# A linear-attention, cosine feed-forward and soft mixture-of-experts chain on one Trainium2 core: 256-column groups taken by pairs in one PSUM bank, and weight conversions and small steps in other slots

## The chip, the cores and the metric

One core of a Trainium2 chip runs the whole program. The metric is device time in microseconds of one execution. The profile adds the time on each engine: TensorE (PE, with PEld for its weight loads), VectorE (DVE), ScalarE (ACT), GpSimd (POOL) and the queue of SyncE (SP), which issues nearly all DMAs.

## The reference, cut to what matters

```python
kv  = einsum('bhsd,bhse->bhde', k, v)          # 8 batches, 8 heads, 576 tokens, 64 dims
out = einsum('bhsd,bhde->bhse', q, kv)
x   = out / sqrt(mean(out*out, -1) + 1e-6) * g_norm        # 4608 tokens x 512
h   = x @ w_in                                              # 512 -> 2048
x   = (h * cos(h)) @ w_out                                  # 2048 -> 512
logits = x @ phi                                            # 32 slots
d = softmax(logits over tokens);  c = softmax(logits over slots)
slot_input = d.T @ x                                        # 8 experts x 4 slots x 512
slot_out[e] = relu(slot_input[e] @ w1[e]) @ w2[e]           # 512 -> 1024 -> 512
return c @ slot_out
```

The inputs w_in and w_out come as 64-bit floats and are rebuilt as 32-bit floats on the core by bit operations.

## The kernel before

**Blocks and slots.** The 4608 tokens are taken in ten blocks (SIZES, L67): blocks 0 to 7 of 512 tokens, blocks 8 and 9 of 256. In each block the 2048 hidden features are 16 groups of 128, and "slot (j, f)" is the place of group f of block j in the program. main (L367) makes one group: 12 matmuls into one of three PSUM banks with the tag h (four steps of 128 rows, each as three products of a high and a low part of w_in and x). In blocks 8 and 9 a group uses 256 of the 512 columns of its bank.

**The chain of a group.** turns (L390, ACT) takes h in turns as an integer, rest (L393, DVE) the fraction, cosine (L397, ACT) the cosine, cos_c (L427, DVE) the product gT = h cos(h) in a buffer of a ring (ring_next, L414). gT then goes two ways. logits (L483) and logits2 (L491, blocks 0 and 1) multiply it with wp, which is w_out times phi. For the slot inputs tokens must be on partitions: either DVE transposes 32x32 squares (L437) and regroup (L468) collects them by DMAs from SP and POOL, or, where on_pe (L363) says so (block 0, half of block 1, the last half of block 9), gtr (L454) transposes on PE and ACT copies. slot_acc (L574) adds up d.T @ g over a block into a PSUM bank "ab". w_out itself is applied only at the end, to the 32 sums.

**The order of the work** is written out by hand. Engines run their instructions in program order. Side work is put at slots by at2 (run after main of that slot), late2 (after the first half of the chain), end2 (after the chain) and ld_at (before main; mostly DMA issues on SP). Two lists of tokens give the start: PLAN["start"] (L36) up to the first group, then PLAN["one"] for slots 0 to 3 of block 0 and PLAN["two"] for the slots in which block 0 and block 1 run side by side (block 1 four slots later). From there a loop (L1075) runs one group after the other.

**Conversions.** For each of 16 groups the steps A (cv_scale, ACT), R, P, L (cv_rest, cv_top, cv_low, all DVE), H (cv_hi, ACT) and S (cv_lo, POOL) rebuild w_in; capital letters in the token lists. Small letters a, r, p, l do the first four for w_out transposed (first written by load_wout, L281), from which wp_kk (L322) and wp_sum (L331) make wp. In slot f the group f + 2 of both is converted (LI and LO, L32 and L33), and wp_kk(f) and wp_sum(f) run in slots f and f + 1. w_in 0 and 1 and w_out 0 and 1 are converted in the start list. logits2 of block 0 run two groups at a time in slots 3, 5, ... 17. In blocks 3 to 6 the steps nat_load to nat_store (L338 to L359) rebuild w_out once more in its natural form and put it in DRAM; four of 16 per block, each with the load two slots ahead of nat_scale (ACT).

**Attention** of block j + 1 is made in block j: kv_pair (L183), att_out (L203: ops matmuls, squares on ACT, sums on DVE, power -0.5 on POOL, L220), att_xs (L223, DVE), att_xT (L231, PE and ACT) and att_lo (L246, DVE). In the start the same steps run for block 0, and for block 1 in slots 1 to 4. All of them use four PSUM banks with the tag at (at_bank, L137), which wps, tr, lr, ab and others share.

**The end of a block.** l_evac, l_add, l_max and l_exp (slots 18 and 19, that is slots 2 and 3 of the next block; l_exp makes ACT load another function table and load the old one back), l_T at 21 and slot_acc at 22 (23 and 26 in block 8).

**Expert weights.** fill and fill_kv (L655, L659) load w1 and w2 (128 pieces of 256 KB) into any buffer that has come free, from slot (7, 8) on to the tail, in a fixed order on SP; load_wo2 reads the natural w_out back. tail (L711) runs the experts and writes 12 output tiles of 768 KB.

Of the kernel before, what the change touches and what calls it, by code (L numbers as in the profile page):

```python
# [46 lines left out]
    lg=6,  # L47
    le=18,
    la=19,
    lx=(3, 1),  # L50
    lT=21,
# [3 lines left out]
    K=((0, (0, 0, 0, 0)), (1, (1, 3, 5, 7)), (1, (10, 12, 15, 18))),  # L55
    KL=(((0, 1), (1, 2), (1, 4), (1, 6)), ((1, 8), (1, 11), (1, 13), (1, 16))),
# [19 lines left out]
def tile_linear_attention__ffn_cos__soft_moe(  # L76
# [76 lines left out]
    def load_q(j, t):  # L153
        if j == 0:
            if t == 0:
                first["q"] = g_p.tile([128, TT[0], 4, 128], F32, tag="g1", name="q")
            q_t[j, t] = first["q"][:, t]
        else:
            q_t[j, t] = q_p.tile([128, 4, 128], F32, tag=f"q{(T0[j] + t) % 3}", name="q")
        nc.sync.dma_start(out=q_t[j, t], in_=qT[T0[j] + t])  # L160

    def load_kv(b, pr):
        if b == 1:
            t = kv_all[:, 1] if pr == 3 else first["kv"][pr]
        else:
            t = kv_all[:, 3 if b in (2, 3) else pr]
# [100 lines left out]
    def stage():  # L267
# [99 lines left out]
    def main(j, f):  # L367
        ps = ps_m.tile([128, 512], F32, tag="h", name="h")[:, 0:SIZES[j]]
# [45 lines left out]
    def ring_next(j, f):  # L414
        if (j, f) == (SMALL, 0):
            ring[:] = [[r[0], r[1][:, a:a + 256], 2 * r[3], r[3]] for k in range(2) for r in ring
                       if r[3] == k and r[2] != 1 for a in (0, 256)]
        i = next(i for i, r in enumerate(ring) if (r[0] not in gT_t or j == NB - 1)
                 and (not r[2] or r[2] == 1 and (j == 0 or j == 1 and f < 10) or r[2] == 2 and (j, f) < (SMALL, 2)))
# [71 lines left out]
    def logits2(j, f):  # L491
        if (j, f) == (0, 0):
# [377 lines left out]
    for j in range(NB):  # L870
# [282 lines left out]
```

## Time and profile before

| | us |
|---|---|
| three runs | 719.93, 721.88, 728.15 (median 721.88) |
| the profiled execution: its own time | 718.57 |
| its span in the profile | 716.6 |
| PE busy in the span | 673.7 (94%) |
| DVE busy | 509.6 (71%) |
| ACT busy | 339.0 (47%) |
| POOL busy | 225.7 (32%) |

Busy shares are averages over stages with different limits. A row of the timeline is a stretch of alike instructions with its start and duration; the chain of waits gives the pieces of the path that ended last; the table by stretches gives busy time, the granted clock of PE (1.00 is the upper level, 0.50 the lower), and the share of time in which the 16 DMA engines were busy. The 1.97 us between span and execution time lie outside what the profile shows.

### The profile page before, as it was taken

To read this page: it belongs to the slowest core of one execution; us is meant where nothing else is said; L and a number is where in the kernel's file an instruction comes from. 1 tells how busy PE (TensorE), PEld (TensorE's weight loads), DVE (VectorE), ACT (ScalarE), POOL (GpSimd) and SP (SyncE) were. 2 spreads that over 40 slices of the span, in tenths; PEclk is the share of its full clock that TensorE was granted. 3 is DMA by queue.
4 is the path that set the end of the run, shared out by engine and by line. 5 is a ranking of instruction groups with operands and counts; after the bars stand their busy time and mean duration, and the time that the engine had idled before them with its cause. 6 is when DMAs were issued, how large, how long until landed. Compare 5 with 4: busy or idle time off the path is not lost.

```text
span 716.6 us, 12698 instructions
## 1 busy us (share of the span) xinstructions
PE 673.7 (94%) x4578; PEld 492.2 (69%) x4578; DVE 509.6 (71%) x941; ACT 339.0 (47%) x635; POOL 225.7 (32%) x337
## 2 busy tenths in 40 slices
PE   7868999999999999999999999999999989799994
PEld 6656777776657776677677677766767768674363
DVE  3896888876577768877887877788776666644144
ACT  3564666634453444445443543543454454551143
POOL 3551111211075343441633333344423513110500
PEclk9998999999999999999999999999999999999996
DMA  9973444212185645764786376455509558999998
GB/s 332 326 245 115 147 160 165 74 44 64 37 196 121 175 133 131 211 150 141 173 236 165 86 194 177 134 150 139 124 15 241 134 185 249 342 340 410 393 394 354
DMA packets 73070, 136.18 MB, mean 190 GB/s; under 512 B 11184, under 2 KB 39472, under 8 KB 72240
## 3 DMA queue, kind: packets, MB, share of 16 engines
q1 hardware_dynamic: 65584, 120.16, 52.6%
q0 software_dynamic: 7424, 15.22, 9.3%
q8 instruction: 36, 0.59, 0.3%
q14 instruction: 26, 0.21, 0.1%
HBM read 91.29 MB, written 13.63 MB: 146 GB/s over the span
## 4 chain that ended last, share of the span: by engine, by line
PE 58%; DVE 18%; DMA 10%; ACT 7%; issue 4%; SPq 1%; POOL 0%; DVEq 0%; ACTq 0%; POOLq 0%
PE h L374 35%; DMA kv<-in_w_out 4%; PE ab L585 4%; DVE gT L427 4%; ACT tmp L397 3%; DVE tmp L393 3%; PE ops L208 3%; DVE tr L437 2%; PE l L488 2%; PE kvps L189 2%; PE eh L737 2%; DVE ss L217 2%; PE tr L457 2%; PE xTps L239 2%; PE l L497 1%
## 5 line engine op out<-in xcount | busy, mean ns | idle before, releaser
L374 PE MATMUL h<-xt,w 128*128 128x512 f32 (+1 forms) x1920 | 427.7, 377 | 11.5 <-DVE gT L427 7.6
L374 PEld LDWEIGHTS h<-xt,w 128*128 128x128 f32 x1920 | 332.7, 190 | 99.3 <-issue 18.3
L397 ACT ACTIVATE tmp<-tmp,hpi 128x512 f32<-128x512 f32 (+1 forms) x160 | 108.8, 681 | 172.5 <-DVE tmp L393 172.4
L476 POOL DMA_DIRECT2D g<-tr x232 | 128.3, 556 | 115.4 <-DVE tr L437 45.6
L427 DVE TENSOR_TENSOR gT<-tmp,h 128x512 f32<-128x512 f32 (+1 forms) x152 | 95.8, 630 | 77.8 <-ACT tmp L397 77.4
L220 POOL TENSOR_TENSOR ri<-ss,mhalf 128x8 f32<-128x8 f32 x36 | 60.0, 1672 | 221.7 <-DVE ss L218 214.8
L393 DVE SCALAR_TENSOR_TENSOR tmp<-h,tmp 128x512 f32<-128x512 f32 (+1 forms) x160 | 99.3, 621 | 23.1 <-ACT tmp L390 22.2
L390 ACT ACTIVATE tmp<-h 128x512 int32<-128x512 f32 (+1 forms) x160 | 87.5, 547 | 54.8 <-PE h L374 53.8
L437 DVE STREAM_TRANSPOSE tr<-gT 128x512 f32<-128x512 f32 (+1 forms) x128 | 84.4, 661 | 6.0 <-DMA g<-tr 0.5
L318 POOL TENSOR_TENSOR w<-st_m,w 128x512 fp32r<-128x512 f32 x16 | 23.7, 1479 | 77.4 <-ACT w L313 77.4
L585 PE MATMUL ab<-g,d 128*32 128x512 f32 x256 | 39.9, 594 | 1.3 <-DVE d L561 1.2
L208 PE MATMUL ops<-kvA,q 128*128 128x128 f32 (+1 forms) x320 | 38.8, 280 | 0.2 <-DVE xt L252 0.2
L208 PEld LDWEIGHTS ops<-kvA,q 128*128 128x128 f32 (+1 forms) x320 | 34.3, 180 | 4.4 <-issue 2.5
L243 ACT ACTIVATE xt<-xTps,gn 128x512 fp32r<-128x512 f32 x36 | 24.4, 683 | 24.6 <-PE xTps L239 23.1
L252 DVE SCALAR_TENSOR_TENSOR xt<-xTps,gn,xt 128x512 fp32r<-128x512 f32 x36 | 26.5, 735 | 7.9 <-ACT xt L243 7.6
L217 DVE TENSOR_REDUCE ss<-sq 128x8 f32<-128x512 f32 x32 | 21.7, 679 | 12.4 <-ACT sq L215 12.3
L585 PEld LDWEIGHTS ab<-g,d 128*32 128x32 f32 x256 | 12.7, 109 | 25.9 <-issue 19.5
L215 ACT ACTIVATE sq<-ops 128x512 f32<-128x512 f32 x32 | 19.1, 596 | 24.0 <-PE ops L208 23.0
L488 PE MATMUL l<-gT,wp 128*32 128x512 f32 (+1 forms) x248 | 30.2, 559 | 0.0
L189 PEld LDWEIGHTS kvps<-kv 128*64 128x64 f32 x464 | 16.0, 137 | 11.2 <-issue 8.6
L227 DVE TENSOR_TENSOR sq<-ops,ri 128x512 f32<-128x512 f32 x32 | 21.5, 677 | 2.4 <-POOL ri L220 2.4
L239 PE MATMUL xTps<-ident,sq 128*128 128x128 f32 x128 | 20.5, 287 | 0.4 <-DVE sq L227 0.4
(159 smaller groups left out, 626.5 us busy)
## 6 DMA issues: line engine op xcount, KB each, us to landing
kv<-in_kv SPq DMA_DIRECT2D x29, 512.0 KB, 6.7
g<-tr SPq DMA_DIRECT2D x232, 64.0 KB, 3.6
g<-tr POOLq DMA_DIRECT2D x232, 64.0 KB, 3.5
ew<-in_w SPq DMA_DIRECT2D x25, 512.0 KB, 9.9
q<-in_qT SPq DMA_DIRECT2D x36, 256.0 KB, 3.7
out<-ot SPq DMA_DIRECT2D x12, 768.0 KB, 6.5
rw<-in_w_in SPq DMA_DIRECT2D x16, 512.0 KB, 5.9
kv<-in_w_out SPq DMA_DIRECT2D x16, 512.0 KB, 8.4
```

What stands on the lines that cost most here:

```text
L208: nc.tensor.matmul(out=ps[p0:p0 + n, pr * 128:(pr + 1) * 128], lhsT=q_t[j, t][:, pr, p0:p0 + n], rhs=kvbd[b % 2][:, pr, :], start=True, st ...
L217: nc.vector.tensor_reduce(out=ss, in_=sq, axis=AX.X, op=ALU.add)
L220: nc.gpsimd.tensor_tensor(out=ri[:, :, 0], in0=ss, in1=mhalf, op=ALU.pow)
L374: nc.tensor.matmul(out=ps, lhsT=w[:, a, kk, :], rhs=x[:, b, kk, :], start=(n == 0), stop=(n == 3 * KD - 1))
L390: nc.scalar.activation(out=t.bitcast(I32), in_=ps, func=AF.Copy, bias=0.25, scale=INV_2PI)
L393: nc.vector.scalar_tensor_tensor(out=t, in0=ps, scalar=INV_2PI, in1=t.bitcast(I32), op0=ALU.mult, op1=ALU.subtract)
L397: nc.scalar.activation(out=t, in_=t, func=AF.Sin, bias=hpi, scale=TWO_PI)
L427: nc.vector.tensor_tensor(out=g, in0=fr, in1=h_t.pop((j, f)), op=ALU.mult)
L437: nc.vector.transpose(out=tr_t[j, q][:, :, i, :], in_=gT_t[j, n * q + i].rearrange("p (b t) -> p b t", t=32))
L476: (nc.gpsimd if b % 2 else nc.sync).dma_start(out=dst[32 * b:32 * b + 32, :, x, a:a + n, :].rearrange("p t f i -> p t (f i)"), in_=src[32 ...
L488: nc.tensor.matmul(out=l_t[j][32 * o:32 * o + 32, :], lhsT=wp[:, f, :], rhs=gT_t.pop((j, f)), start=(c == 0), stop=(c == (2 if j == NB - 1 ...
L585: nc.tensor.matmul(out=ps[32 * c:32 * c + 32, :], lhsT=d[:, t, :], rhs=gs[c // 2][t][:, (c % 2) * 512:(c % 2) * 512 + 512], start=(t == 0) ...
```

## The change

What it does:

- Blocks 8 and 9: groups f and f + 1 (f even) share one PSUM bank, 256 columns each. Both mains run, each with its loads and side work, then one chain of 512 columns makes both gT. One DVE instruction transposes both. The ring keeps its 512-column buffers, and both tmp buffers stay in use to the end, so the fill of tmp1 moves from (8, 5) to the tail.
- w_out conversions: no small letters are left in the start list. Group w is converted in slot co[w], from 3 to 13, with two groups in slots 5, 7, 9, 11 and 13. wp_kk and wp_sum follow 2 and 3 slots later, logits2 of block 0 in slots l0. Four gT of block 0 get buffers in the unused half of the q tile.
- Start: the first w_in tile is loaded ahead of k and v, and converted before the first kv_pair; w_in 1 after the last att_lo instead of between them.
- Blocks 2 to 7: the last logits at slot 17 instead of 18, evacuation, maximum, exponential and l_T one slot earlier each (block 7: l_T at 23, slot_acc at 26).
- The natural w_out: three groups per block in blocks 3 to 6 and four in block 7, loads three to seven slots ahead of nat_scale. Loads of q, k and v, fills of kv_all and the regroup of block 8 move by some slots.

The diff, cut to its core:

```diff
-    wT=0,
-    wM=1,
+    co=(3, 4, 5, 5, 6, 7, 7, 8, 9, 9, 10, 11, 11, 12, 13, 13),
+    l0=(8, 9, 10, 12, 13, 15, 16, 17),
...
     start=(
-        "lkv.2 rem.0 lkv.1 lkv.0 lkv.3 q.0 win.0 wout.0 win.1 win.2 warm.12 wout.1 lkv.4 lkv.6 lkv.5 kv.1 kv.2 "
-        "kv.0 kv.3 ao.0 ao.1 ao.2 ao.3 lkv.7 xs.0 A.0 warm.4 R.0 xT.0 P.0 rem.1 xs.1 L.0 wout.2 xT.1 q.1 "
-        "lo.0 xs.2 A.1 H.0 S.0 warm.4 a.0 lo.1 xT.2 xs.3 warm.4 R.1 P.1 lo.2 xT.3 r.0 win.3 a.1 L.1 lo.3 H.1 r.1 "
-        "p.0 S.1 p.1 l.0 l.1 "
+        "win.0 lkv.2 rem.0 lkv.1 lkv.0 lkv.3 q.0 win.1 lkv.4 lkv.6 win.2 lkv.5 A.0 R.0 P.0 L.0 H.0 S.0 warm.12 kv.1 kv.2 kv.0 "
+        "kv.3 lkv.7 rem.1 q.1 win.3 wout.0 wout.1 wout.2 ao.0 ao.1 ao.2 ao.3 A.1 xs.0 warm.4 xT.0 xs.1 lo.0 "
+        "warm.4 xT.1 xs.2 lo.1 warm.4 xT.2 xs.3 lo.2 xT.3 lo.3 R.1 P.1 L.1 H.1 S.1 "
     ),
...
-    lg=6,
-    le=18,
-    la=19,
-    lx=(3, 1),
-    lT=21,
+    lg=(6, 10, 14, 17),
+    le=17,
+    la=18,
+    lx=(2, 1),
+    lT=20,
...
-    kv=(14, 14, 18, 18),
-    kvl=10,
+    kv=(14, 14, 17, 17),
+    kvl=(9, 10, 13, 14),
...
-    nt=((3, 2), (3, 6), (4, 2), (4, 6), (5, 2), (5, 6), (6, 2), (6, 6)),
+    nt=((1, 4, 0, 0), (2, 7, 1, 1), (3, 10, 3, 0), (9, 13, 0, 1)),
...
+        tq = g_p.tile([128, 4096], F32, tag="g1", name="q")
+        ring[:0] = [[None, tq[:, 2048 + TB * i:2048 + TB * (i + 1)], 3, 0] for i in range(4)]
...
+        if j >= SMALL:
+            gT_t[j, f], gT_t[j, f + 1] = g[:, 0:256], g[:, 256:512]
+            if not on_pe(j, f):
...
+                nc.vector.transpose(out=tr_t[j, q][:, :, o:o + 2, :].rearrange("p b f t -> p f b t"),
+                                    in_=g.rearrange("p (f b t) -> p f b t", f=2, t=32))
+            return
...
-                        ld_at(j, (9, 17)[q] + i, regroup, j, q, (2 * i, 2 * i + 1))
+                        ld_at(j, ((11, 17) if j == SMALL else (9,))[q] + i, regroup, j, q, (2 * i, 2 * i + 1))
...
-                at2(0, f + PLAN["wT"], wp_kk, f)
-                at2(0, f + PLAN["wM"], wp_sum, f)
+                at2(0, PLAN["co"][f] + 2, wp_kk, f)
+                at2(0, PLAN["co"][f] + 3, wp_sum, f)
...
-    for i in range(4):
-        ld_at(7, 8 + i, fill_kv, i)
+    for u in range(NF):
+        n, i = (3 + u // 3, u % 3) if u < 12 else (7, u - 12)
+        a, f, slot, half = PLAN["nt"][i]
+        ld_at(n, a, nat_load, u, slot, half)
+        at(n, f, nat_scale, u)
+        late(n, f, nat_bits, u)
+        end(n, f, nat_low, u)
+        ld_at(n, f + 2, nat_store, u)
+    for i, f in ((1, 9), (3, 12), (0, 15), (2, 17)):
+        ld_at(7, f, fill_kv, i)
...
-        for j, f in [(1, f) for f in range(NF - L, NF)] + [(j, f) for j in range(2, NB) for f in range(NF)]:
+        for j, f in [(1, f) for f in range(NF - L, NF)] + [(j, f) for j in range(2, SMALL) for f in range(NF)]:
...
+        for j, f in [(j, f) for j in range(SMALL, NB) for f in range(0, NF, 2)]:
+            ps = ps_m.tile([128, 512], F32, tag="h", name="h")
+            for i in range(2):
+                run(loads, j, f + i)
+                main(j, f + i, ps[:, 256 * i:256 * i + 256])
+                run(side, j, f + i)
+            h_t[j, f] = ps
+            cos_a(j, f)
+            for i in range(2):
+                run(post, j, f + i)
+            cos_b(j, f)
+            cos_c(j, f)
+            for i in range(2):
+                run(fin, j, f + i)
```

## Rows read from the trace of the kernel before

**Rows 1.** Who PE waited for, whole run: us, times, longest.

```profile
PE h L374 <- DVE gT L427: 7.6, 7, 3.2
PE tr L457 <- DVE sq L227: 4.1, 1, 4.1
PE wps L326 <- DVE sq L227: 3.1, 1, 3.1
PE ldT L559 <- DVE ld L542: 2.4, 1, 2.4
```

**Rows 2.** Table by stretches: span, busy time per engine, PEclk, DMA share, GB/s.

```profile
42.00:60.00 18.00, 10.55 (x66) 7.56 (x66) 14.24 (x25) 7.86 (x17) 7.54 (x5) 0.83 0.53 185
94.34:102.26 7.92, 7.92 (x52) 6.01 (x51) 6.95 (x11) 5.33 (x14) 1.30 (x1) 1.00 0.45 159
```

**Rows 3.** Chain of waits, start: k and v landing, and the first group.

```profile
3.37 6.65 DMA kv<-in_kv
...
25.92 4.38 PE h L374 x11
```

**Rows 4.** Timeline of the start: the four powers of block 0 on POOL.

```profile
13.69 6.99 POOL L220 TENSOR_TENSOR ri<-ss,mhalf 128x8 f32<-128x8 f32 x4 [11.47 <-DVE ss L218]
```

**Rows 5.** Chain of waits, slots 3 to 6 of block 0.

```profile
57.69 1.69 PE l L497 x4
...
63.12 5.67 PE h L374 x24
...
69.72 0.84 PE l L497 x4
...
78.01 0.14 PE wps L333 x2
78.16 0.36 PE wps L326 x8
...
85.56 0.86 PE l L497 x8
```

**Rows 6.** Groups by line, 63 to 134 us: the conversions on DVE.

```profile
L302 DVE SCALAR_TENSOR_TENSOR st<-st 128x512 int32<-128x512 int32 x9 | 13.3, 1483 | 0.0
L307 DVE SCALAR_TENSOR_TENSOR st<-st 128x512 int32<-128x512 int32 x9 | 6.6, 735 | 0.0
L302 DVE SCALAR_TENSOR_TENSOR st_m<-rw,st_m 128x512 int32<-128x512 int32 x9 | 6.2, 693 | 0.3
L297 DVE TENSOR_SCALAR st<-st 128x512 int32<-128x512 int32 x9 | 3.8, 421 | 0.1
```

**Rows 7.** Line L345 (nat_scale): what ACT waited for, us and times.

```profile
  DMA kv<-in_w_out: 10.5, 4
```

**Rows 8.** Timeline: one chain of 512 columns, up to its transposition.

```profile
563.11 0.60 ACT L390 ACTIVATE tmp<-h 128x512 int32<-128x512 f32 x1 [1.32 <-PE h L374]
563.74 0.69 DVE L393 SCALAR_TENSOR_TENSOR tmp<-h,tmp 128x512 f32<-128x512 f32 x1 [0.48 <-ACT tmp L390]
...
565.94 0.71 DVE L437 STREAM_TRANSPOSE tr<-gT 128x512 f32<-128x512 f32 x1
```

**Rows 9.** Timeline of blocks 8 and 9: the chains of 256 columns, and PE unhindered.

```profile
589.98 3.12 PE L374 MATMUL h<-xt,w 128*128 128x256 f32 x24
...
595.53 0.39 DVE L393 SCALAR_TENSOR_TENSOR tmp<-h,tmp 128x256 f32<-128x256 f32 x1
...
597.31 0.39 DVE L393 SCALAR_TENSOR_TENSOR tmp<-h,tmp 128x256 f32<-128x256 f32 x1
...
635.79 0.39 ACT L390 ACTIVATE tmp<-h 128x256 int32<-128x256 f32 x1
...
637.22 0.42 DVE L427 TENSOR_TENSOR gT<-tmp,h 128x256 f32<-128x256 f32 x1 [0.57 <-ACT tmp L397]
```

**Rows 10.** Table by stretches of 5 us, late: the last two columns are DMA.

```profile
585.00:590.00 5.00, 5.00 (x43) 3.68 (x32) 4.20 (x9) 1.44 (x4) 0.72 (x1) 1.00 0.00 2
...
605.00:610.00 5.00, 4.70 (x39) 3.74 (x38) 2.98 (x8) 2.23 (x6) 3.23 (x7) 1.00 0.95 335
```

More of the change, by code (lines that the diff above doesn't have):

```diff
@@ L163, in load_kv @@
         if b == 1:
-            t = kv_all[:, 1] if pr == 3 else first["kv"][pr]
+            t = first["kv"][pr]
         else:
@@ L271, in stage @@
         first["wi"] = [wi[:, i, :] for i in range(2)]
-        first["wo"] = [tc_[:, 512 * i:512 * i + 512] for i in range(3)]
+        first["wo"] = [tc_[:, 512 * i:512 * i + 512] for i in range(2)] + [A]
         first["wq"] = [ta[:, 1536 + 128 * i:1664 + 128 * i] for i in range(2)]
@@ L364, in on_pe, with main @@
         return j == 0 or j == 1 and f < NF // 2 or j == NB - 1 and f >= NF // 2
-    def main(j, f):
-        ps = ps_m.tile([128, 512], F32, tag="h", name="h")[:, 0:SIZES[j]]
+    def main(j, f, ps=None):
+        if ps is None:
+            ps = ps_m.tile([128, 512], F32, tag="h", name="h")
         w, x = w_t[f], xt_t[j]
@@ L415, in ring_next @@
         if (j, f) == (SMALL, 0):
[L416 to L419, printed above, removed]
+            ring[:] = [r if r[3] == 0 else r[:2] + [2, 1] for r in ring if r[2] == 0]
+            ring.sort(key=lambda r: r[3])
+        i = next(i for i, r in enumerate(ring) if (r[0] not in gT_t or j == NB - 1) and (
+            not r[2] or r[2] == 1 and (j == 0 or j == 1 and f < 10) or r[2] == 3 and j == 0 and f < 4
+            or r[2] == 2 and (j, f) < (SMALL, 2)))
         r = ring.pop(i)
@@ L491, in logits2 @@
     def logits2(j, f):
-        if (j, f) == (0, 0):
+        if "a" not in l_t:
             l_t["a"] = ps_l.tile([128, TB], F32, tag="l", name="l")
@@ L890, in tile_linear_attention__ffn_cos__soft_moe @@
                 late_in = j and f + 3 + L >= NF - (L < 6)
[L891 removed]
+                at2(*((1, f + 3) if late_in else (0, f + 3 + L if j else PLAN["l0"][f // 2])), logits2, j, f)
         if j < NB - 1:
             for c in range(4 * (j > 1)):
[L894 to L895 removed]
+                at2(j, 4 * c + 6 if j == SMALL else PLAN["lg"][c], logits, j, c)
+            le, la, lx, how = (PLAN["E"][j] if j < 2 else (18, 19, 3, 1) if j == SMALL
+                               else (PLAN["le"], PLAN["la"], *PLAN["lx"]))
             at2(j, le, l_evac, j)
@@ L946, in tile_linear_attention__ffn_cos__soft_moe @@
         for pr in range(4):
-            sl = PLAN["KL"][b - 2] if b < 4 else [(b - 2, PLAN["kvl"] + x) for x in range(4)]
+            sl = PLAN["KL"][b - 2] if b < 4 else [(b - 2, x) for x in PLAN["kvl"]]
             ld_at(*sl[pr], load_kv, b, pr)
@@ L959, in load_wo2 @@
         wo2[n] = t
-    for g, (n, f) in enumerate(PLAN["nt"]):
-        for i in range(2):
-            u = 2 * g + i
-            ld_at(n, f + i, nat_load, u)
-            at(n, f + 2 + i, nat_scale, u)
-            late(n, f + 2 + i, nat_bits, u)
-            end(n, f + 2 + i, nat_low, u)
-            ld_at(n, f + 4 + i, nat_store, u)
-    for i in range(4):
-        ld_at(7, 8 + i, fill_kv, i)
+    for u in range(NF):
[8 more added lines that the diff above has]
+        ld_at(7, f, fill_kv, i)
     ld_at(7, 8, fill, rem_p, "vr", 1)
@@ L974, in tile_linear_attention__ffn_cos__soft_moe @@
     ld_at(8, 5, fill, gt_p, "gt1", 3)
-    ld_at(8, 5, fill, const, "tmp1", 1)
     for i in range(3):
@@ L1030, in token @@
             out = int(k.islower())
-            w = int(arg[0]) if arg else f + (PLAN["LO"] if out else PLAN["LI"])
-            if w < NF and (arg or w >= (PLAN["PO"] if out else PLAN["PI"])):
-                ck(k.upper(), w, out)
-                steps[k.upper()](w, out)
+            ws = [int(arg[0])] if arg else [w for w in range(NF) if PLAN["co"][w] == f] if out else [f + PLAN["LI"]]
+            for w in ws:
+                if w < NF and (arg or out or w >= PLAN["PI"]):
+                    ck(k.upper(), w, out)
+                    steps[k.upper()](w, out)
         elif arg:
@@ L1069, in tile_linear_attention__ffn_cos__soft_moe @@
                 ld_at(0, f, load_win, f + PLAN["LI"] + 2)
-            if f + PLAN["LO"] + 1 < NF and f + PLAN["LO"] + 1 + NF not in loaded:
-                ld_at(0, f, load_wout, f + PLAN["LO"] + 1)
+            if f > 2:
+                ld_at(0, PLAN["co"][f - 3] + 1, load_wout, f)
         for f in range(NF):
@@ L1091, in tile_linear_attention__ffn_cos__soft_moe @@
                 fill(const, "tmp0", 1)
+                fill(const, "tmp1", 1)
                 fill(gt_p, "gt0", 3)
```

43 lines of the change are left out of this document (20 added, 23 removed).

## The prediction

> **What bounds the kernel now.** I read in this order: who PE waited for, the table by stretches, the chain of waits, and the timeline of the stages that the change touches. The list of PE's waits [rows 1] is short for a span of 716.6 us: PE is the bound nearly everywhere, so an edit is worth what it takes from PE's waits or from PE's own work. The reader is to see where these few waits lie. Two, 3.1 and 4.1 us, are in slots 2 and 3 of block 0; that stretch of 18.00 us has PE busy for only 10.55, and its clock at 0.83 [rows 2]. The seven waits of main for gT add up to 7.6: one of 3.2 in block 9, while ACT exchanges tables, the other 4.4 in blocks 3 to 6. The 2.4 of ldT is in block 8. A steady slot of two groups is the other picture: 7.92 us, PE busy throughout, DVE for 6.95 [rows 2]. At the end the DMAs bound: idle at 585 us, they are busy for 0.95 of the time from 605 us on [rows 10], and stay so while weights come in and outputs go out.
>
> All sums are made against the profiled execution, 718.57 us. The three runs lie 1.4 (lowest) to 9.6 us above it, their median 3.3. I put the forecast on the scale of ordinary runs by adding 1.4.
>
> **Start, up to the second group.** win.0 (512 KB, one DMA issue on SP) now goes ahead of everything. Four tiles of the same size were on their way for 6.65 us [rows 3], 1.66 each, so k and v come later by 0 (if the transfers were not the limit) to 1.66; I take 1.5. Behind them is a chain that this does not shorten: four powers in a row on POOL, 6.99 us [rows 4], ending at 20.68. From there to the first full group at 25.92 [rows 3] are 5.2 us, in which DVE now also does conversions of w_in 0 and 1 and of w_out. These go, but the new list places xT of each tile behind lo of the tile before. The gain here is between 0 and 5.2 less 1.5; I take 1.5, so the start comes out at 0. The eleven matmuls at 4.38 [rows 3] ran at the lower level of the clock behind such a wait, and I expect them to do so again.
>
> **Slots 0 to 4.** Here DVE is late: it carries two conversions per slot, and xs of block 1 stands behind them. Taken away are the w_out conversions of five groups, with 2.64 us of DVE each (1.483 + 0.735 + 0.421) [rows 6]. PE loses, before the mains of slot 4 at 63.12 [rows 5], five wp_kk (0.36), four wp_sum (0.14) and one logits2 at the low clock (1.69): 1.80 + 0.56 + 1.69 = 4.0. Of the waits of 7.2 us not all can go: xs needs two powers per slot, half of 6.99, and these come after main, so what is late next is POOL. I let half of the waits stay: 3.6 gained, from bounds of 0 and 7.2. The lower clock in this stretch costs at most half of 0.34 x 18 = 6.1 us, that is 3.1; I count 0.5 of it. Sum: 8.1 by slot 4.
>
> **What comes back.** The same PE work is now done at full clock, in slots where PE is the bound and nothing hides it. wp: 5 x 0.36 + 4 x 0.14 = 2.4. logits2: eight matmuls of blocks 0 and 1 together take 0.86, four alone 0.84 [rows 5]. Before, from slot 7 on both blocks shared their slots; with l0, slots 8, 10, 12 and 16 hold block 0 alone, and 7 and 11 block 1 alone. That is ten places instead of eight, of which the one in slot 3 is already counted: 3 x 0.84 = 2.5. Back: 4.9.
>
> **DVE in slots 5 to 13.** Fourteen conversions stand in nine slots where nine stood. Each of the five extra ones costs DVE 2.64, or 1.85 if only the first of two meets POOL (0.693, the step of w_in, in place of 1.483) [rows 6]: 9.3 to 13.2 us. Free is 9 x (7.92 - 6.95) = 8.7, plus the 4.9 by which PE gets longer: 13.6. It fits on average, but not in a slot with two: 6.95 + 2.64 = 9.6 against about 8.5. Three banks of h let the chain lag by a group and a half, so most of it is ridden out. I take 1.5 of waits; bounds 0 and 5 x (9.6 - 8.5) = 5.5, with the clock left out. ACT's part of the extra conversions costs nothing, as ACT is busy for 5.33 of 7.92 [rows 2]; w_out loads are issued a slot behind the conversion that frees their buffer, three groups ahead, and w_in loads stay where they were.
>
> What the row shows of this contention is 1.483 for the step that runs beside POOL's, 0.693 for the same instruction apart from it [rows 6]. The Trainium skill (SBUF — State Buffer, "Who interferes with whom") says that a DVE instruction with two inputs in SBUF and a GpSimd one that reads SBUF exclude each other for the whole instruction. By that rule only the first of two steps in a slot pays, and the extra work is 9.3; by the row's mean it is 13.2. The trace agrees with such a block, POOL having 1.30 us in such a slot [rows 2], and I lean to the lower end.
>
> Block 0 and 1 together: 8.1 - 4.9 - 1.5 = 1.7.
>
> **Blocks 2 to 7.** In four blocks ACT stood waiting for a w_out tile, 10.5 us in all [rows 7], with the next group's turns queued behind it; DVE and PE follow. Loads now stand three to seven slots ahead instead of two, and three instead of four conversions share a block. I take 3.3 of the 4.4 us of PE's waits; bounds 0 and 4.4. Block 7 gets four conversions: PE had no wait there, and if this cover is gone it costs what one of the blocks 3 to 6 lost, 1.1. SP now issues the third kv load behind the store that frees its buffer; regroups queue behind it, but their readers come slots later: 0. Last logits one slot earlier: gT of group 15 is ready 2.83 us after its main (563.11 to 565.94) [rows 8], and two mains of 2.8 (half of 5.67) [rows 5] lie between: 0, at worst 0.3 per block. The exponential, l_T and q loads move with no reader closer than before: 0.
>
> **Blocks 8 and 9.** Where nothing else is on PE, DVE and ACT in turn set the pace: from one rest to the next 1.78 us per group (595.53 to 597.31), while PE needs 3.12 / 2 = 1.56 [rows 9]. A pair's chain takes 2.91 (563.74 to the end of the transposition at 566.65) [rows 8] against PE's 3.12 [rows 9]: PE becomes the bound. Three banks now hold six groups, so the table exchange is covered. In block 8 the bounds are 0 and 2.4 [rows 1] + 16 x 0.22 = 5.9; much of the second part is hidden by other PE work now, so I take 2.5. In block 9 up to 3.2 [rows 1] + 8 x 0.22 = 5.0 goes. But a wait is added: gtr(f) now follows the main of the next pair's first group, and gT is ready only 2.83 after the pair's second, so PE waits 2.83 - 1.56 = 1.27, with the next main queued behind it. Three pairs, and the last chain 2.83 instead of 1.85 (635.79 to 637.64) [rows 9]: 3.8 + 1.0 = 4.8. Net 0. More would not be kept anyway, as the DMAs bind from there on [rows 10]. The fills follow block 8's slots, so its 2.5 stay. tmp1's 256 KB at the end lie among loads that are queued: 0.
>
> **Sum.** 1.7 + 3.3 + 2.5 = 7.5; 718.57 - 7.5 = 711.1; as an ordinary run 712.5 us.
>
> **The rivals** (times as ordinary runs).
>
> A, the other side: DVE binds in the five double slots, and PE's waits bring its clock down, as from 42 to 60 us. For: 9.6 us of DVE against 8.5; the clock fell behind waits of 3 to 4 us. Against: the average fits. It decides from 9.0 us on (all gains, with the 1.5 already counted), 1.8 per double slot; at 2.5 per slot 12.5 are lost in place of 1.5: 723.5.
>
> B: slots 2 and 3 wait for POOL, not for DVE. Then the 7.2 us stay, the start is 1.5 later, 4.0 goes and 4.9 comes back, 1.5 is lost: -3.9 + 3.3 + 2.5 = 1.9; 718.1. For: powers fill half of the time between the sums and xs. Against: DVE is busy for 14.24 of 18 us there [rows 2].
>
> C: the covers hold everywhere: start 2 better, waits and clock 4 better, no DVE waits (1.5), blocks 3 to 6 whole (1.1), block 8 half of the rest (1.7): about 10 more, 702 to 707.
>
> D: pairs bring nothing. The chain starts only after both groups, so in block 8 too PE waits, and the DMAs hide the rest: 2.5 to 5 less, 715 to 717.5. The trace shows no reader of h beside a writer of the same bank. The Trainium skill (PSUM — Partial Sum Buffer, "PSUM bank collisions raise a hardware error") has two engines kept off one bank even at different columns; by it an earlier start for the first half is not to be had, and D's wait is sure, its cover not.
>
> **Numbers.** Forecast 0.46, A 0.09, B 0.18, C 0.13, D 0.14. A measurement of this kernel tells about 1% from no change, 7.2 us: under 714.7 is faster. That is C, nearly all of the forecast and a little of D: 0.57. Slower by over 1% is part of A: 0.07. The rest, 0.36. The range, 705 to 722, leaves out the far ends of A and C; the forecast alone spans 708 to 716.
>
> **What would show it.** Right: PE's waits in slots 2 and 3 at about 3.6; the slots from 5 on at about 8.5 us; no wait of ACT for w_out; no wait of ldT or of main for gT in blocks 8 and 9, but about 1.3 of tr for gT three times. Wrong: double slots over 9.5 us with a clock under 1.00, a first group after 27 us, or a longer stretch from block 8's end to the end of the span.

## The result, and the profile after

The changed kernel takes 728.7 us (median of 20 runs, 725.7 to 732.6), the kernel before 722.2 (20 runs, 718.8 to 728.2). The ratio is 1.0082, with a 95% interval of 1.0056 to 1.0108: slower by some 6 us. The forecast was 712.5, its range 705 to 722. Below, ratios are to the kernel before on the same chip, with their 95% interval; a time "on the scale of 722.2" is the ratio times 722.2. The profiled execution of the changed kernel spans 727.3 us, that of before 716.6, which is at the low end of its runs.

Who PE waited for in the changed kernel, whole run (us, times, longest), to be set beside [rows 1]:

```profile
PE xTps L234 <- DVE sq L222: 17.1, 4, 12.2
PE tr L465 <- DVE gT L426: 5.2, 3, 1.8
PE wps L324 <- ACT g L138: 3.5, 2, 2.1
...
PE h L373 <- DVE gT L426: 1.4, 5, 0.3
```

The waits of main for gT, 7.6 before, are down to 1.4, as wanted. One wait of 12.2 us is new, longer than any sum in [rows 1]. The row names DVE, but that is only the last link. PE waits for xs (L222) of block 9's second tile; DVE waits for ACT; ACT stands here (timeline of ACT and PE, block 8):

```profile
569.10 0.72 ACT L396 ACTIVATE tmp<-tmp,hpi 128x512 f32<-128x512 f32 x1
581.32 0.69 ACT L238 ACTIVATE xt<-xTps,gn 128x512 fp32r<-128x512 f32 x1 [11.49 <-DMA ew<-in_w]
...
588.62 1.09 PE L234 MATMUL xTps<-ident,sq 128*128 128x128 f32 x4 [12.18 <-DVE sq L222]
```

ACT writes xt of block 9 at slot (8, 5). That tile has the tag T2 (att_xT), and T2 last held the transposed groups that block 7's last regroup reads. So ACT waits until those DMAs have read it. They come late (the DMA queue of SP, same stretch):

```profile
569.76 0.33 SPq L654 DMA_DIRECT2D kv<-in_w  x1
570.13 2.08 SPq L654 DMA_DIRECT2D ew<-in_w  x3
572.26 2.76 SPq L484 DMA_DIRECT2D g<-tr  x4
```

The four DMAs of the second half of the regroup (g<-tr) are issued at 572.26, behind the fill of kv_all's third part, for which SP had to wait 1.2 us until the store of w_out had read that buffer, and behind x1 (2 MB). Before, the same four and the same xt stood so:

```profile
571.76 2.84 SPq L476 DMA_DIRECT2D g<-tr  x4
...
581.84 0.69 ACT L243 ACTIVATE xt<-xTps,gn 128x512 fp32r<-128x512 f32 x1 [1.42 <-DMA ew<-in_w]
```

The times of the issue and of xt are nearly the same in both kernels; PE is what has moved. ACT was free for xt at 569.8 after the change, at 580.4 before, where it waited only 1.42 us. What PE had gained in blocks 2 to 7 it stood still for.

The table by stretches shows what follows:

```profile
42.00:60.00 18.00, 14.01 (x84) 11.41 (x88) 15.98 (x27) 10.66 (x19) 7.96 (x6) 1.00 0.39 128
...
570.00:580.00 10.00, 6.44 (x56) 5.49 (x54) 1.25 (x2) 0.00 (x0) 0.00 (x0) 1.00 0.94 310
580.00:590.00 10.00, 1.38 (x7) 1.42 (x8) 6.39 (x12) 3.85 (x7) 1.64 (x1) 0.58 0.20 69
590.00:600.00 10.00, 10.00 (x80) 6.77 (x80) 2.94 (x5) 2.04 (x4) 2.03 (x4) 0.91 0.10 21
```

ACT does nothing for ten microseconds, PE stops behind it at the transposition shown above and is busy for 1.38 of 580 to 590, and the granted clock falls to 0.58 there. The last two columns matter as much: from 580 to 600 the DMAs are nearly idle. SP stands there for 13.6 us at block 8's regroup, for a transposition of DVE that comes late, with all later fills behind it. In the first line (slots 2 and 3), PE is busy for 14.01 of 18 us where it was 10.55, at full clock [rows 2]: that part of the forecast came true.

The end of both kernels (sT, the slot inputs ready for the experts, and the output DMAs on SP), first before, then after:

```profile
653.81 0.98 PE L725 MATMUL sT<-rep,part 128*128 128x32 f32 x8
...
688.59 20.45 SPq L792 DMA_DIRECT2D out<-ot  x12
```

```profile
662.85 0.98 PE L733 MATMUL sT<-rep,part 128*128 128x32 f32 x8
...
699.10 21.60 SPq L800 DMA_DIRECT2D out<-ot  x12
```

These two marks carry the rest of the study: sT is how far PE has come, the first output is how far PE and the weights together have come.

### The profile page after: what moved, and what is told of

It reads as the page before. It is cut to its first block, busy times and chain, and to the rows that moved or that the text cites. A ratio compares the mean times of both kernels' runs of the same rounds, so it can differ in the third digit from the quotient of the medians.

```text
span 727.3 us, 12628 instructions
## 1 busy us (share of the span) xinstructions
PE 672.8 (93%) x4578; PEld 493.0 (68%) x4578; DVE 500.9 (69%) x897; ACT 334.5 (46%) x603; POOL 222.3 (31%) x337
## 4 chain that ended last, share of the span: by engine, by line
PE 67%; DMA 12%; ACT 9%; DVE 8%; issue 2%; SPq 1%; POOL 0%; DVEq 0%; ACTq 0%; POOLq 0%
PE h L373 44%; DMA ew<-in_w 5%; PE ab L593 4%; PE ops L203 4%; PE l L496 3%; ACT tmp L396 2%; PE kvps L184 2%; PE xTps L234 2%; DMA g<-tr 2%; PE fo L797 2%; PE l L505 2%; DVE gT L426 2%; DMA kv<-in_w2h 1%; DMA kv<-in_w 1%; ACT L544 1%
## 5 line engine op out<-in xcount | busy, mean ns | idle before, releaser
L396 ACT ACTIVATE tmp<-tmp,hpi 128x512 f32<-128x512 f32 x144 | 104.0, 724 | 166.4 <-DVE tmp L392 166.2
L426 DVE TENSOR_TENSOR gT<-tmp,h 128x512 f32<-128x512 f32 x134 | 91.6, 685 | 68.5 <-ACT tmp L396 68.2
L392 DVE SCALAR_TENSOR_TENSOR tmp<-h,tmp 128x512 f32<-128x512 f32 x144 | 97.1, 675 | 40.9 <-ACT tmp L389 39.9
L389 ACT ACTIVATE tmp<-h 128x512 int32<-128x512 f32 x144 | 85.1, 591 | 66.2 <-PE h L373 66.0
L445 DVE STREAM_TRANSPOSE tr<-gT 128x512 f32<-128x512 f32 x103 | 73.1, 711 | 4.0
L316 POOL TENSOR_TENSOR w<-st_m,w 128x512 fp32r<-128x512 f32 x16 | 21.3, 1330 | 85.8 <-ACT w L311 85.8
L203 PEld LDWEIGHTS ops<-kvA,q 128*128 128x128 f32 (+1 forms) x320 | 34.8, 180 | 5.1 <-issue 3.3
L593 PE MATMUL ab<-g,d 128*32 128x512 f32 x256 | 33.3, 593 | 0.8 <-DMA g<-tr 0.8
L234 PEld LDWEIGHTS xTps<-ident,sq 128*128 128x128 f32 x128 | 15.0, 142 | 23.3 <-issue 15.0
L184 PEld LDWEIGHTS kvps<-kv 128*64 128x64 f32 x448 | 16.6, 147 | 12.7 <-issue 9.8
L593 PEld LDWEIGHTS ab<-g,d 128*32 128x32 f32 x256 | 9.5, 110 | 21.1 <-issue 19.3
```

The lines of the kernel that those rows point to most:

```text
L203: nc.tensor.matmul(out=ps[p0:p0 + n, pr * 128:(pr + 1) * 128], lhsT=q_t[j, t][:, pr, p0:p0 + n], rhs=kvbd[b % 2][:, pr, :], start=True, st ...
L234: nc.tensor.transpose(ps[:, kk * 128:(kk + 1) * 128], xs[:, kk * 128:(kk + 1) * 128], ident)
L389: nc.scalar.activation(out=t.bitcast(I32), in_=ps, func=AF.Copy, bias=0.25, scale=INV_2PI)
L392: nc.vector.scalar_tensor_tensor(out=t, in0=ps, scalar=INV_2PI, in1=t.bitcast(I32), op0=ALU.mult, op1=ALU.subtract)
L396: nc.scalar.activation(out=t, in_=t, func=AF.Sin, bias=hpi, scale=TWO_PI)
L445: nc.vector.transpose(out=tr_t[j, q][:, :, i, :], in_=gT_t[j, n * q + i].rearrange("p (b t) -> p b t", t=32))
```

## Experiments

### What the wait costs

e1: two fills behind the regroup.

```diff
-    ld_at(8, 1, fill, x_p, "x1", 8)
+    ld_at(8, 4, fill, x_p, "x1", 8)
-    for i, f in ((1, 9), (3, 12), (0, 15), (2, 17)):
+    for i, f in ((1, 9), (3, 12), (0, 15), (2, 19)):
```

> The changed kernel, but the fill of x1 (2 MB) goes from slot (8, 1) to (8, 4) and the fill of the third part of kv_all from (7, 17) to (7, 19), so that both stand behind block 7's last regroup on SP. Main theory (regroup queue): block 9's first xt lies in tile T2, which that regroup still reads; ACT waited 11.5 us for it at 569.8 to 581.3 and PE 12.2 us, with the clock at 0.50 afterwards. Then the wait falls under 2 us and the time falls by 9 to 12 us, from 728.7 to 717 to 720. Rival 1 (the pairs themselves): the chain of 512 columns and the transposition on PE cost the time, and the wait only moves on: 725 to 729. Rival 2 (the weight loads bound the end): x1 filled later makes the last weights land later, and the time stays at 727 to 730 although the wait at (8, 5) is gone.

Measured: 0.9966 [0.9934, 0.9997], on the scale of 722.2 some 719.7. Two moved lines take 1.16% (8.4 us) off the changed kernel. The wait of ACT for a DMA is gone, PE's wait there is 3.2 instead of 12.2 (under 2 was expected), and sT stands at 654.06 instead of 662.85. The main theory holds for the wait; its 9 to 12 us were a little too many. Which of the two lines counts more was not tried. Part of the gain is lost at the end, where the output starts at 692.11: 38.1 us after sT, against 34.8 before. There the weights are late, which is what rival 2 spoke of.

e2: the changed kernel with single groups in blocks 8 and 9. e3: with the old start and conversions. (Each puts the lines of the kernel before back.)

> The changed kernel with blocks 8 and 9 by single groups of 256 columns as before; start, conversions and blocks 2 to 7 stay as changed. Main theory (regroup queue): block 8 still begins some 7 us earlier than before, so ACT still waits 9 to 11 us for the regroup at (8, 5); only the end of block 9 changes, by 2 to 5 us: 723 to 727. Rival 1 (the pairs themselves cost it): 714 to 718.

> The kernel before with the pairs and the changed blocks 2 to 7, but with its own start, conversions and logits of blocks 0 and 1. From the two profiles blocks 0 and 1 lost 4 to 5 us by the change (slot (2, 0) at 184.1 instead of 180.4). Theory A (that loss reaches the end): 723 to 725. Theory B (block 8 waits for transfers that don't follow): the lead is lost in the wait at (8, 5), 727 to 729.

Measured: e2 1.0051 [1.0030, 1.0072], e3 1.0048 [1.0019, 1.0076]; 2.2 and 2.5 us better than the changed kernel, which is within the intervals. Neither removes the wait: 6.0 us of ACT in e2 (9 to 11 were expected), and in e3

```profile
ACT xt L243 <- DMA g<-tr: 12.3, 1, 12.3
```

Here the trace names the regroup itself (g<-tr). e3's old start is 3 us faster at block 2, and its wait 0.8 longer, with xt only 0.2 us earlier. For e2 the main theory's time holds, for e3 the measured 725.7 lies between A and B.

e4: the pairs alone on the kernel before.

> The kernel before with the pairs of blocks 8 and 9 alone. Main theory (regroup queue): block 8 begins when it did before, so PE comes to (8, 5) only some 1.5 us earlier, and the wait there grows from 1.4 to about 3 us; block 8 gains about 1, the end of block 9 loses up to 5: 721 to 726 against 722.2. Rival 1 (the pairs themselves cost it): 727 to 733.

Measured: 1.0051 [1.0028, 1.0075], 725.9: the upper end of the main theory. ACT waits 5.9 us at (8, 5), where some 3 were expected, PE 5.2 for the transpositions. Counted from block 6's slot_acc (at 533.62 in this profile, 530.48 in that of before), ACT is free for xt 3.3 us sooner with the pairs, and xt starts 1.2 us later: both lengthen the wait.

e10: blocks 2 to 7 alone, and e7: the same with e1's two lines.

> The kernel before with the changed blocks 2 to 7 alone, x1 at (8, 1) and the third part of kv_all at (7, 17) as in the changed kernel. Main theory (regroup queue): block 9's first xt waits 6 to 11 us for block 7's last regroup, and PE with it: 720 to 724, that is 4 to 7 over the run with the late fill (716.4 on the scale of 722.2). Theory E in its strong form (the stream lags 7 us there anyway and hides the wait): 716 to 718.

> The kernel before with the changed blocks 2 to 7 and, as in the run with the late fill, x1 at (8, 4) and the third part of kv_all at (7, 19); start and the single groups of 256 columns as before. Theory D (blocks 2 to 7 bring 10 us by themselves, and the wait at (8, 5) took them): 711 to 715. Theory C (weights bound the end, and this part moves 3 MB of w_out and the first fills to later places): 717 to 721.

Measured: e10 1.0022 [0.9985, 1.0059], e7 0.9920 [0.9890, 0.9951]. The same two lines are worth 1.0% (7.4 us) here too, without pairs and with the old start. So the largest part of the change gains 5.8 us, or nothing, by the place of two fills; the main theory holds (723.8). But the wait of ACT in e10 is only 6.0 us, half of that in e3, though PE is 9.6 us earlier at block 6's slot_acc than before (520.91 against 530.48): xt starts at 575.81, not at 581. In e6 below, where PE is later than before, ACT still waits 3.0 us. First e10, then e6:

```profile
575.81 0.69 ACT L243 ACTIVATE xt<-xTps,gn 128x512 fp32r<-128x512 f32 x1 [5.99 <-DMA ew<-in_w]
...
589.92 0.69 ACT L238 ACTIVATE xt<-xTps,gn 128x512 fp32r<-128x512 f32 x1 [3.02 <-DMA ew<-in_w]
```

So the date at which T2 is free is not fixed. In the nine profiles with x1 ahead of the regroup, xt starts 6.3 to 9.0 us after the last regroup DMA has been issued on SP; in the three with x1 behind it whose trace puts a wait of ACT down to the regroup (e13, e14, e15), 2.1 to 2.8 us. So x1 in front costs more after the issue (3.5 us at the least) than in the issue itself (2.08 us in the changed kernel). D's 711 to 715 for e7 fell: the gain of PE is there, but not all of it at the end, 716.4.

### What the end waits for

e5: the changed kernel without the last 4.2 MB of weights.

```diff
-    todo += [(4 + i, 1, h, a, n) for h in (1, 2) for a, n in ((0, 4), (4, 2), (6, 2)) for i in range(4)]
+    todo += [(4 + i, 1, h, a, n) for h in (1,) for a, n in ((0, 4), (4, 2), (6, 2)) for i in range(4)]
...
-                                     rhs=GR.pop((4 * G + i, 1, h, r)), start=(r == 0), stop=(r == 7))
+                                     rhs=GR[4 * G + i, 1, min(h, 1), r], start=(r == 0), stop=(r == 7))
```

> The changed kernel without the last 32 pieces of w2 (128 KB each, 4.2 MB): their matmuls take the pieces of the first half of the columns in their place, so the second half of the columns isn't computed from its own weights. Every matmul stays. Theory C (weights bound the end: from 645 us on the DMA share is 0.95 to 1.05 at some 405 GB/s in every profile, and SP issues the first output only when the last weights are issued): 4.2 MB are 10.4 us of that stream, so the time falls by 7 to 10 us, from 728.7 to 718 to 722, by as much as PE lets it. Rival (PE's chain bounds the end, the transfers lie beside it): 727 to 729.

Measured: 1.0103 [1.0068, 1.0138], 729.6, no gain. Theory C in this form is refuted: the DMAs are busy from 645 us on in every profile, yet here an eighth of the weights (16 of 128 pieces of 256 KB) could go for nothing:

```profile
690.00:700.00 10.00, 9.64 (x91) 5.21 (x85) 1.69 (x4) 2.77 (x6) 0.00 (x0) 1.00 0.42 153
```

The DMA share falls to 0.42 and PE is still busy for 9.64 of 10. From sT to the first output this profile has 36.1 us, the changed kernel 36.2. In the changed kernel the end is nearly all PE's chain, because PE is so late; only pieces ahead of these can still count, as in e17 below, where that stretch is 33.3. A full DMA column alone doesn't say that DMAs bound the end.

e9: e7 with ten pieces of the weights (2.5 MB) earlier.

```diff
-    ld_at(7, 8, fill, rem_p, "vr", 1)
-    ld_at(7, 9, fill, rem_p, "kr", 2)
+    ld_at(6, 1, fill, rem_p, "vr", 1)
+    ld_at(6, 1, fill, rem_p, "kr", 2)
...
-        ld_at(8, 12, fill, q_p, f"q{i}", 1)
-    ld_at(8, 12, fill, const, "kvA", 2)
+        ld_at(8, 7, fill, q_p, f"q{i}", 1)
+    ld_at(8, 7, fill, const, "kvA", 2)
...
-        ld_at(8, 15, fill, a_p, "a", 1)
+        ld_at(8, 10, fill, a_p, "a", 1)
```

> The run of blocks 2 to 7 with the late fill, and ten more pieces (2.5 MB) earlier: vr and kr at (6, 1) instead of (7, 8) and (7, 9), the three q tiles and kvA at (8, 7) instead of (8, 12), the two a tiles at (8, 10) instead of (8, 15). In that run PE had the slot sums ready 11 us earlier than before (sT at 642.8 instead of 653.8), but the second layer of the experts took 31.0 us instead of 24.0 because the weights came late. Theory E (two chains, PE up to sT and the weight stream, and here the stream is the later one): 2.5 MB at 405 GB/s are 6.2 us, so the time falls by 4 to 6 us, 711 to 713. Rival (the second layer is PE's or the output's): 715 to 718.

Measured: 0.9890 [0.9810, 0.9970], 714.3, with a wide interval, between E (711 to 713) and the rival (715 to 718) and not told apart from e7 by it. The output starts at 683.55 instead of 684.17: the pieces came earlier, and later ones still waited for buffers.

e8: the natural w_out four groups per block in blocks 3 to 6 again, with all else as in e1 but the fills of kv_all back at (7, 8) to (7, 11).

```diff
-    nt=((1, 4, 0, 0), (2, 7, 1, 1), (3, 10, 3, 0), (9, 13, 0, 1)),
+    nt=((1, 3, 0, 0), (2, 5, 1, 1), (3, 7, 3, 0), (4, 8, 0, 1)),
```

> The changed kernel with the fill of x1 at (8, 4), and the natural w_out rebuilt four groups per block in blocks 3 to 6 as before, loads at slots 1, 2, 3 and 4, scales at 3, 5, 7 and 8, so that block 7 has none and the fills of kv_all go back to (7, 8) to (7, 11). Theory C (weights bound the end): the first fills land some 10 us earlier and 3 MB less are moved in block 7, so the time falls below the run with the late fill by 2 to 5 us: 716 to 719. Rival (the moved fills don't matter, and shorter leads bring back the waits of ACT in blocks 3 to 6): 721 to 726.

Measured: 1.0073 [1.0041, 1.0105], 727.5. The rival's time, and more than it said. PE's waits for gT in blocks 2 to 7 are back, and at nat_scale (L343) ACT stands again; first PE's row, then what ACT waited for:

```profile
PE h L373 <- DVE gT L426: 9.5, 10, 2.4
...
  DMA wo_dr<-kv: 15.6, 4
```

But this isn't the rival's mechanism. Before, ACT waited for loads (10.5 us, [rows 7]); here it waits for stores. The fourth group's scale at slot 8 writes over the half of kv_all that the second group's store, issued at slot 7, is still reading. So e8 says what such a wait costs (9.5 us of PE against 1.4 in the changed kernel), not what three groups per block or longer leads bring. For that there are the profiles of the changed kernel, e7 and e10: no wait of ACT at nat_scale, and waits of main for gT in blocks 2 to 7 of 1.4 us and less.

### The start

e6: the changed start, conversions and logits of blocks 0 and 1 alone.

> The kernel before with the changed start, conversions and logits of blocks 0 and 1 alone. In the profile of the changed kernel block 2 began 3.8 us later for them. Theory A (a lag of PE reaches the end whole): 725.5 to 727 against 722.2. Theory C (the end is the weight stream's, and what PE loses early is partly made up in blocks 2 to 7, where waits are shorter when it comes later): 722 to 724.5.

Measured: 1.0048 [1.0010, 1.0087], 725.7. Theory A: the lag of 3.8 us reaches the end, as far as an interval from 0.7 to 6.3 us can tell. e15 (the changed kernel with single groups and e1's two lines, so that only the start stands between it and e7) says the same:

> The changed kernel with single groups of 256 columns in blocks 8 and 9 and the late fill. Against the run of blocks 2 to 7 with the late fill (716.4) only the start is changed. Theory A (the start's lag reaches the end whole): 719 to 721. Rival (block 2 makes it up, since in the changed kernel block 7 ended only 0.9 us later than with the old start): 716 to 718.

Measured: 0.9978 [0.9947, 1.0009], against 0.9920 for e7: 4.2 us.

e12: e6 with the logits of block 0 beside those of block 1.

```diff
-    l0=(8, 9, 10, 12, 13, 15, 16, 17),
+    l0=(7, 9, 10, 11, 13, 15, 15, 17),
```

> The kernel before with the changed start alone, but the logits of block 0 in slots 7, 9, 10, 11, 13, 15, 15, 17 instead of 8, 9, 10, 12, 13, 15, 16, 17, so that they stand beside those of block 1 in all but one slot; two matmuls alone took 1.04 us, four together 0.86. Theory F (the unshared logits are a part of PE's loss in blocks 0 and 1): three stretches fewer, 2 to 3 us: 722.5 to 724 against 725.7. Rival (ACT's chain sets those slots, PE waits in its place): 725 to 727.

Measured: 1.0038 [0.9997, 1.0078]: 0.7 us below e6, well within both intervals. The edit took only 1.2 us out of PE's work on the logits (11.38 to 10.20 from slot 5 to slot 16) and added 1.1 of waits for wp, so the 2 to 3 us of theory F weren't there to be gained. It doesn't tell whether the logits count.

### The pairs

e11: e7 with the pairs. e13: e11 with three transpositions one slot later.

```diff
-                at2(j, f + (1 if j == 1 and f < NF // 2 else 2), gtr, j, f)
+                at2(j, f + (1 if j == 1 and f < NF // 2 else 3 if j == NB - 1 and f in (8, 10, 12) else 2), gtr, j, f)
```

> The run of blocks 2 to 7 with the late fill, and the pairs in blocks 8 and 9. The pairs alone cost 0.5% on the kernel before. Theory E (stream later than PE): PE's sums come 4 to 5 us later for the waits of the transpositions (5.2 us) and the longer last chain, and the stream's lag of 7 us hides most of it: 716 to 718. Rival (the pairs cost the same 3.6 us wherever they stand): 719.5 to 721.

> The run of pairs with blocks 2 to 7 and the late fill, but the transpositions on PE of groups 8, 10 and 12 of block 9 one slot later, beside those of 9, 11 and 13, behind one more main of 1.56 us. Theory G (PE's three waits of 1.64 to 1.82 us for gT are part of what the pairs cost): the waits fall from 5.2 to under 1 us and the time by 2 to 4 us, from 720.3 (0.9973 of 722.2) to 716 to 718.5. Rival (the wait comes back elsewhere, or the weights hide it): 719 to 721.

Measured: e11 0.9973 [0.9943, 1.0003], e13 0.9982 [0.9947, 1.0017]. The pairs cost 3.8 us here as well, as the rival of e11 had it, and moving the transpositions brings nothing. Yet the step that theory G named did go: PE's wait of tr falls from 5.2 to 0.4 us. First e11, then e13:

```profile
649.95 0.98 PE L734 MATMUL sT<-rep,part 128*128 128x32 f32 x8
...
687.95 21.01 SPq L801 DMA_DIRECT2D out<-ot  x12
```

```profile
643.50 0.98 PE L734 MATMUL sT<-rep,part 128*128 128x32 f32 x8
...
688.47 19.54 SPq L801 DMA_DIRECT2D out<-ot  x12
```

sT comes 6.5 us earlier in the one profile, the output no earlier: there the weights are the later chain, and from 660 to 680 PE is busy for 16.6 of 20 us. With e5 this gives both sides of one picture: the end is the later of PE's chain and the stream of weights. In the changed kernel PE is later, in e13 the weights.

e14: e7 with pairs in block 8 alone (in block 9 the old single chain, with the ring and the tmp buffers cut in halves). e16: the same with e9's earlier pieces; e18 repeats it.

> The run of blocks 2 to 7 with the late fill, and pairs in block 8 alone; block 9 goes by single groups of 256 columns as before. Theory H (block 8 gains by pairs, as forecast, and all of the loss is block 9's): 713.5 to 716 against 716.4 without pairs and 720.3 with pairs in both. Rival (block 8 loses too, or gains nothing): 717 to 719.

> The run with ten pieces of the weights earlier, and pairs in block 8 alone. If what pairs gain in block 8 and what the earlier pieces gain add up: 711 to 714. If the pairs' loss is in block 8 too, or the weights still bound the end: 715 to 718.

Measured: e14 0.9964 [0.9931, 0.9998], 719.6, above both expectations; e16 0.9840 [0.9767, 0.9913], 710.6, below both. What e14's profile shows of this is in its queue and PE's waits:

```profile
561.74 7.93 SPq L487 DMA_DIRECT2D g<-tr  x8
569.71 0.60 SPq L657 DMA_DIRECT2D kv<-in_w  x1
```

```profile
PE xTps L239 <- DVE sq L227: 6.8, 2, 5.3
```

Even with the two fills behind it, the regroup needs 7.93 us to be issued, ending at 569.67, ACT waits 4.5 us for it, and PE 5.3 again. But this execution took 723.0 us, near the top of e14's runs (715.5 to 723.5). And up to block 9 the program of e14 is that of e11 and e13, where ACT waits for the regroup 0 and 3.8 us. So with the fills behind it the wait comes and goes from one execution to another, and why e14 is slower than e7 is not shown. In e16, where vr and kr are gone from block 7, the same eight DMAs are issued from 557.44 to 564.00, and the largest wait of PE left there is 1.5 (2.3 in e18). Its output starts at 677.65, the earliest of all.

e17: the changed kernel with e1's and e9's moves.

> The changed kernel with the late fill and the ten earlier pieces of the weights; start, conversions and pairs in both blocks as changed. With the late fill alone it took 0.9966 of before. Theory E (two chains, PE up to sT and the weight stream): the wait of 3.2 us left at (8, 5) goes, since vr and kr no longer stand in the queue of block 7, and the stream's 3 to 4 us too: 0.987 to 0.992, 713 to 716.5. Rival (the start's lag and the waits of the transpositions on PE bound it): 0.994 to 0.997, 718 to 720.

> The best version once more, for its interval: blocks 2 to 7 as changed, late fill, ten pieces earlier, pairs in block 8 alone, start as before. If the 0.984 of three rounds holds: 0.980 to 0.988. If it was a lucky chip: 0.988 to 0.992, like the run of early loads without pairs.

Measured: e17 0.9874 [0.9829, 0.9918], 716.2 us as median; e18 0.9773 [0.9730, 0.9816], below the 0.980 to 0.988 that were expected, 707.8 us as median of its runs (e16: 709.1). The kernel before had a median of 725.5 beside e17 and e18, of 721.1 beside e16, so the medians compare better than the ratios here. e18 beats both kernels: blocks 2 to 7 as changed, the old start, pairs in block 8 alone, and ten fills issued at other places. And the changed kernel itself, with nothing but these fills moved (e17), is by the medians 12.5 us faster than it was; by the time, rival and theory E are told apart there, for E. Of E's two terms the profile shows one: sT to the first output falls from 38.1 us (e1) to 33.3, the weights; PE's wait at (8, 5), which was to go, is still 3.1 us (3.2 in e1).

## Why the prediction was wrong

**The step that failed** is the sentence on blocks 2 to 7: "regroups queue behind it, but their readers come slots later: 0". It asked who reads what a regroup writes, and not who writes over what it reads. That is the first xt of block 9, in T2. The trace of before held the row: ACT's xt waited 1.42 us for a DMA. So a date hung on SP's queue, and ACT was already ahead of it by 1.4 us. That date moved less than PE did: with PE 9.6 us earlier at block 6's slot_acc (520.91 in e10, 530.48 before), xt starts 6.0 earlier; in the changed kernel, with PE 6.5 earlier there and the pairs behind it, 0.5 earlier. The wait was worth 8.4 us (e1) and 7.4 us (e10 and e7). None of the rivals had it; A, the one on the other side, was another mechanism.

The Trainium skill (DMA: Bandwidth & Descriptors, "Anatomy of one DMA — SWDGE (gpsimd) path") says that DMA engines don't wait on semaphores, and that any such wait is taken by the issuing sequencer before dispatch. The trace of SP's queue agrees: SP stands from 568.50 to 569.76 for one buffer, and everything behind it waits along.

**Blocks 2 to 7** were predicted at 3.3 us and gained over 10. PE at slot (2, 0), then slot_acc of blocks 3 and 6, first before (the weight loads of the last one with it), then after:

```profile
180.36 5.51 PE L374 MATMUL h<-xt,w 128*128 128x512 f32 x23 [0.69 <-DVE xt L252]
...
339.51 4.83 PE L585 MATMUL ab<-g,d 128*32 128x512 f32 x32 [0.42 <-DVE d L561]
...
530.43 0.16 PEld L585 LDWEIGHTS ab<-g,d 128*32 128x32 f32 x2 [0.68 <-DVE d L561]
530.48 4.89 PE L585 MATMUL ab<-g,d 128*32 128x512 f32 x32
```

```profile
184.11 5.52 PE L373 MATMUL h<-xt,w 128*128 128x512 f32 x23 [0.68 <-DVE xt L247]
...
340.66 3.62 PE L593 MATMUL ab<-g,d 128*32 128x512 f32 x32
...
523.95 3.62 PE L593 MATMUL ab<-g,d 128*32 128x512 f32 x32
```

From 3.75 us behind to 6.53 ahead: 10.3. Waits for gT went from 4.4 to 1.4, 3.0 of it, about as forecast (3.3), and the waits for d themselves make 1.2. The other large term was priced at 0: l_T one slot earlier. Before, the 32 matmuls of slot_acc started behind a wait for d, of PE or of its weight loads, and took 4.83 to 4.93 us; after, d is ready, and the same 32 take 3.62. In blocks 2 to 6 that is 6.2 us, which no list of waits shows, as PE counts as busy.

**Slots 2 and 3** came out as predicted: 1.7 + 1.7 = 3.4 us of waits left, 3.6 forecast, with 1.3 more in slot 4. The first full group came 1.8 us later and was faster: eleven matmuls in 2.79 us from 27.73, at full clock, where the forecast had half clock. Slot 5 began at 60.31 instead of 70.50. The step that failed is "what comes back", with the double slots. The stretch from slot 5 to the first half of slot 16, before and after:

```profile
70.50:157.79 87.29, 87.29 (x599) 68.11 (x597) 74.78 (x119) 54.51 (x122) 16.30 (x12) 1.00 0.35 121
```

```profile
60.31:160.36 100.05, 95.12 (x632) 71.15 (x629) 80.86 (x134) 59.68 (x136) 16.70 (x12) 0.98 0.37 127
```

12.8 us are lost there, not 6.4 (4.9 of work and 1.5 of waits): PE's work grew by 7.8, and 4.9 it stood. The work that was undersized is that of the logits (table by stretches for their line alone, before and after):

```profile
70.50:157.79 87.29, 6.31 (x42) 1.33 (x40) 1.00 0.35 121
```

```profile
60.31:160.36 100.05, 11.38 (x44) 2.24 (x44) 0.98 0.37 127
```

They grew by 5.1 us where 2.5 were forecast; wps grew from 7.3 to 10.0, 2.7 for 2.4. The waits are not rival A's either: those that the list names are PE's for ACT's copies, 3.5 of wps and 1.1 of l. The slot that begins at 68.24 took 10.33 us with DVE busy for 10.23, but PE's own work there is 9.21 and its one wait the 1.1 for a copy, so that DVE is the bound in the double slots is not shown. Net for blocks 0 and 1 (another 1.2 us go after slot 16): minus 3.8 instead of plus 1.7; e6 and e15 measure 3.5 and 4.2 at the end.

**Blocks 8 and 9.** The waits for transpositions were foreseen, at 1.27 each, and measured 1.64 to 1.82. The last chain was undersized: from the last main to ldT the trace shows 7.2 us (646.09 to 653.29), before 4.9 (639.33 to 644.19), 2.3 more where 1.0 was added. "The DMAs bind from there on" was half true: they bind when PE is early enough (e13), and not in the changed kernel (e5). By the runs the pairs cost 3.7 us (e4) and 3.8 (e11).

**The sum.** Alone, the start costs 0.48%, the pairs 0.51%, blocks 2 to 7 with the wait 0.22%; together 1.21%, measured 0.82%. With 0.24% to 0.39% on either side of each part this is not told from a plain sum. Set against the forecast, in us gained: blocks 0 and 1 1.7 forecast and -3.5 measured (e6); blocks 2 to 7 3.3 and, without the wait, 5.8 (e7); blocks 8 and 9 2.5 and -3.7 (e4); the wait for the regroup 0 and -7.4 (e10 against e7).

**Open.** Of the start's loss the logits are measured as work but no run takes them out (e12 hardly did), and why ACT's copies come late is not shown. The pairs' loss in block 9 was not tried without those in block 8. What puts SP's queue, and with it the landing of the regroup, later in one kernel than in another is not isolated. Why e16 gains so much more over e14 than e9 over e7 (1.2% against 0.3%) is not shown either: e16's profile has the wait at (8, 5) gone and the stretch from sT to the first output at 35.1 us instead of 43.7, while in e9 that stretch stayed at 41.0 (e7: 41.4).

## What to carry to other kernels

Before a gain is booked, look for the dates downstream that do not move with it, or move less: for each tile that a stage writes, find the last DMA that reads what lay in it, where that DMA stands in its queue, and how many bytes are ahead of it. A wait there, even of 1.4 us, says that no margin is left. And price an earlier operand by the consumer's duration too, not only by its wait.

## What the runs showed of the hardware

- 32 matmuls into four 32-row strips of a bank took 3.62 us when their operand was ready, and 4.83 to 4.93 when they started behind a wait for it: the first weight loads then went in by twos instead of fours, and the later ones did not catch up. In the five blocks in which this changed, 6.2 us.
- The tile that a regroup of four DMAs reads was free 6.3 to 9.0 us after the last of them was issued when a 2 MB fill stood ahead of it in the queue, and 2.1 to 2.8 us after when that fill stood behind.
- Issuing one regroup DMA on SP took 0.69 us where four took 2.76, and 1.0 where eight took 7.93, while other transfers filled the queue. So the issue time of such a DMA is not a constant.
- From 650 to 700 us both kernels moved 398 to 400 GB/s with a DMA share of 1.02 to 1.03, and still 4.2 MB less did not shorten the changed kernel.
